# Top-32 attention with a mixture of experts: the second candidate list is sorted down to eight, and three of nine segments give five candidates to the first list

## The chip, the cores and the metric

The kernel runs on one core of one Trainium2 chip. The metric is device time in microseconds (us) of one execution, the median of several runs. Time before: 373.49 us, the median of 3 runs (372.68 to 374.3). A core has a matrix engine (TensorE, PE in the rows, with its weight loads as PEld), a vector engine (VectorE, DVE), a scalar engine (ScalarE, ACT), GpSimd (POOL), SyncE (SP, which issues DMAs here), and 16 DMA engines. Each engine works through its own queue in order and waits on semaphores.

## What is computed

Attention in which each row keeps its 32 largest scores, and then a mixture of experts with one expert per token (8 experts, 1152 tokens):

```
scores = scale * np.matmul(q, k.transpose(0, 1, 3, 2))          # 2 batches, 8 heads, 576 x 576, head size 64
kth = np.partition(scores, -top_k, axis=-1)[..., -top_k:-top_k + 1]   # top_k = 32
scores = np.where(scores >= kth, scores, -1000000000.0)
attn = softmax(scores)
x = np.matmul(attn, v)                     # as 1152 tokens x 512
expert_idx = np.argmax(x @ w_gate, axis=1)
y = np.maximum(x_e @ w1[e], 0.0) @ w2[e]   # per expert e, for its tokens; times the gate's probability
```

## The kernel before

**Units.** Attention is cut into 36 units `u`: 9 tiles of 128 query rows times 4 pairs of heads. A unit holds two score tiles (j = 0, 1) of 128 x 576 in PSUM. Four units make one tile of tokens, which is then routed to the experts.

**How 32 of 576 are found.** `heads` (L285) cuts each row's 576 scores into nine segments of 64 and takes the eight largest of each, sorted, with one MAX8 per segment (L292, 18 per unit), into `un`. The first four of each segment form the first list (36 values), the last four the second list (36 values). `merge` (L299) needs the 16 smallest of the first list and the 16 largest of the second: MAX8 for eight of them (L295 and L305 for the second list into `vb`, L309 for the first into `na`; the first list is read from `nn`, a negated copy), MATCH_REPLACE8 to strike these eight out (L312 second, L315 first; each is a MATCH_VALUE_LOAD and a MATCH_REPLACE8 on the engine), and MAX8 again for the next eight (L317 second, L319 first). With both lists sorted, the 32nd largest of their union is the largest of the minima of pairs: `bound` (L323, in four steps L326, L328, L330, L332) takes twelve pairs per row. Where that bound leaves more than 32 scores above it, up to seven too many are taken away later: `select` (L371) reads the eight smallest kept values with one MAX8 over the row (L380) and picks the threshold.

**Who does what in a unit.** DVE runs `heads`, a reduction that gives the row's maximum (`mx`, L296), `select` of an older unit, and `merge`. ACT makes `nn` from `un` (L336), copies the scores out of PSUM as `sm` = maximum minus score (L339, needs `mx`), takes the exponentials (L417, L408), makes the mask `pen` (L394, needs `nk`, which DVE's L384 writes at the end of `merge`) and the signs that count the kept scores (L349). PE transposes (L415, L416, L406, L407), multiplies by v (L437, L440) and computes the next unit's scores (L277), into the same PSUM tiles that ACT's `sm` copy has to leave first. POOL multiplies for `select` (L356) and splits weights (L616, L618).

**What sets the order.** The order is written by hand. `attention` (L1028) walks over the units; in step i it runs `heads` of unit i, and work of units i-1 to i-9 around it. Small DVE steps (`bound`, parts of `select`, `normalise` L445 with L451, L453, L456 of every second unit, the routing steps) stand in a list `small` and are put between the MAX8 of `heads` and inside `merge`, one at each call of `fill`. In every fourth unit ACT also copies the transposed tokens (L505) and PE runs the gate (L508). After the last unit, from about 240 us, comes the experts' part, bound by weight splits and matrix products.

A repair branch at the end of the program runs the exact selection for everything if any row's bound left fewer than 32 or more than 39 scores.

Of the kernel before, what the change touches and what calls it, by code (L numbers as in the profile page):

```python
# [27 lines left out]
LOW = -3.0e38  # L28
TOPK = 32
SEG = 9  # L30
SPLIT = 256.0


@with_exitstack
def kernel(
# [117 lines left out]


    pd = psum.tile([128, 512], FT, name="pD", bufs=1)
    NB = [pd[:, 24 * i:24 * i + 24].rearrange("p (j c) -> p j c", j=2) for i in range(2)]
    DM = [pd[:, 64 + 16 * i:80 + 16 * i].rearrange("p (j c) -> p j c", j=2) for i in range(2)]
    M1 = [pd[:, 96 + 2 * i:98 + 2 * i] for i in range(2)]
    tab = pd[:, 104:112]
    CG = pd[0:1, 128:256].rearrange("p (i c e) -> p i c e", i=4, c=4)  # L160
    nc.vector.tensor_scalar(tab, e_f, 2.0, float(2 * TOPK - S), op0=OP.mult, op1=OP.add)
    VB = [consts.tile([128, 2, 17], FT, name=f"vb{i}") for i in range(2)]
    for vb in VB:
        nc.vector.memset(vb[:, :, 0:1], -LOW)
    CNT = consts.tile([128, NT * H], FT)
# [114 lines left out]
    def scores_of(u, j):  # L280
        return PS[u][j][:, :S]
# [1 line left out]


    def heads(u, fill):  # L285
        un = work.tile([128, 2, SEG, 8], FT, name="un")
        nn = work.tile([128, 2, SEG, 4], FT, name="nn")
        mx = work.tile([128, 4, 2], FT, name="mx4", bufs=3)
        w = S // SEG
        for j in range(2):  # L290
            for i in range(SEG):
                nc.vector.max(out=un[:, j, i], in_=scores_of(u, j)[:, i * w:(i + 1) * w])  # L292
                if i < SEG - 1:
                    fill()
        nc.vector.max(out=VB[u % 2][:, 0, 1:9], in_=un[:, 0, :, 4:])  # L295
        nc.vector.tensor_reduce(out=mx[:, 0], in_=un[:, :, :, 0], axis=mybir.AxisListType.X, op=OP.max)  # L296
        VAL[u] = [mx, un, nn]

    def merge(u, fill):  # L299
        mx, un, nn = VAL[u]  # L300
        wk = work.tile([128, 2, 2, SEG, 4], FT, name="wk")
        na = work.tile([128, 2, 16], FT, name="na")
        tm = work.tile([128, 2, 12], FT, name="tm")
        vb = VB[u % 2]
        nc.vector.max(out=vb[:, 1, 1:9], in_=un[:, 1, :, 4:])  # L305
        if u == NU - 1:
            fill()
        for j in range(2):
            nc.vector.max(out=na[:, j, 0:8], in_=nn[:, j])  # L309
        fill()  # L310
        for j in range(2):
            nc.vector.match_replace(out=wk[:, 0, j], in_to_replace=vb[:, j, 1:9], in_values=un[:, j, :, 4:],  # L312
                                    imm_value=LOW)
        for j in range(2):
            nc.vector.match_replace(out=wk[:, 1, j], in_to_replace=na[:, j, 0:8], in_values=nn[:, j], imm_value=LOW)  # L315
        for j in range(2):
            nc.vector.max(out=vb[:, j, 9:17], in_=wk[:, 0, j])  # L317
        for j in range(2):
            nc.vector.max(out=na[:, j, 8:16], in_=wk[:, 1, j])  # L319
        fill()  # L320
        VAL[u] = [mx, na, vb, tm]

    def bound(u, step):  # L323
        mx, na, vb, tm = VAL[u]
        if step == 0:
            nc.vector.tensor_scalar(NB[u % 2], na[:, :, 4:16], -1.0, None, op0=OP.mult)  # L326
        elif step == 0.5:
            nc.vector.tensor_tensor(out=tm, in0=NB[u % 2], in1=vb[:, :, 0:12], op=OP.min)  # L328
        elif step == 1:
            nc.vector.tensor_reduce(out=M1[u % 2], in_=tm, axis=mybir.AxisListType.X, op=OP.max)  # L330
        else:
            nc.vector.tensor_sub(mx[:, 2], mx[:, 0], M1[u % 2])  # L332


    def shift(u):
        nc.scalar.activation(VAL[u][2], VAL[u][1][:, :, :, :4], AF.Copy, scale=-1.0)  # L336
        SM[u] = work.tile([128, 2, S], FT, name="sm", tag="sm", bufs=4)
        for j in range(2):
            nc.scalar.activation(SM[u][:, j], scores_of(u, j), AF.Identity, bias=VAL[u][0][:, 0, j:j + 1],  # L339
# [1019 lines left out]
```

## Time and profile before

| what | value |
| --- | --- |
| median of 3 runs | 373.49 us |
| the profiled execution | 375.27 us, of which the span of the program is 373.4 us |
| PE busy | 326.8 us, 88% of the span |
| DVE busy | 321.1 us, 86% |
| ACT busy | 291.9 us, 78% |
| POOL busy | 273.2 us, 73% |

Busy time is a union of an engine's instructions over the whole span; the stages differ, so the shares are to be read per stage. On DVE an instruction's time in the trace overlaps with the next one's start, so what an instruction costs its queue is the distance from its start to the start of the next, and this is the number used below. A figure in brackets at the end of a row is the idle time of that engine just before the instruction, with what ended it.

### The profile page before, as it was taken

How to read it: one execution, taken by the hardware profiler on the slowest of the kernel's cores; microseconds unless marked ns; L12 is line 12 of the kernel's file. 1: busy time of each engine (PE TensorE's matmuls, PEld its weight loads, DVE VectorE, ACT ScalarE, POOL GpSimd, SP SyncE). 2: the span in 40 equal slices, each digit the busy share in tenths (PEclk: the TensorE clock that was granted, in tenths of full speed). 3: DMA queues.
4: the chain of work that ended last, by engine and by line, in shares of the span. 5: the costliest groups of instructions: out<-in, count | busy, mean ns of one | idle time of the engine just before them, and what ended most of it. 6: DMA issues, size and time to landing. Idle time of an engine off the chain costs nothing.

```text
span 373.4 us, 10232 instructions
## 1 busy us (share of the span) xinstructions
PE 326.8 (88%) x3390; PEld 269.4 (72%) x3390; DVE 321.1 (86%) x1863; ACT 291.9 (78%) x573; POOL 273.2 (73%) x293
## 2 busy tenths in 40 slices
PE   5777888988988889888799998999899999898892
PEld 2455666866777768667688887999358978877781
DVE  4889999999999999999999999877863679879820
ACT  5789999999999999998979987765745776677410
POOL 3895969698977789989879999774602578578431
PEclk9778999999999999999989999999999999999897
DMA  9739997936283403030323015394279999999110
GB/s 156 132 72 202 223 196 221 218 113 158 49 254 127 176 32 115 3 141 2 113 58 116 2 37 143 122 351 172 77 224 317 367 324 326 401 334 285 42 32 25
DMA packets 69924, 60.27 MB, mean 161 GB/s; under 512 B 52069, under 2 KB 52069, under 8 KB 69863
## 3 DMA queue, kind: packets, MB, share of 16 engines
q1 hardware_dynamic: 67719, 54.79, 53.7%
q0 software_dynamic: 1616, 4.73, 3.4%
q8 instruction: 28, 0.46, 0.5%
q14 instruction: 33, 0.27, 0.2%
q10 hardware_dynamic: 528, 0.02, 0.1%
HBM read 40.66 MB, written 12.09 MB: 141 GB/s over the span
## 4 chain that ended last, share of the span: by engine, by line
DVE 50%; PE 36%; ACT 5%; issue 4%; DMA 2%; POOL 1%; SPq 1%; POOLq 0%; ACTq 0%
DVE un L292 17%; DVE z L380 10%; PE pS L656 8%; PE pV L440 5%; PE pT L656 4%; PE pD L656 3%; DVE ws L618 3%; DVE wk L315 2%; DVE wk L312 2%; PE pS L277 2%; PE pT L415 2%; PE pT L738 2%; ACT ws L612 2%; DVE vb L317 2%; DVE na L309 1%
## 5 line engine op out<-in xcount | busy, mean ns | idle before, releaser
L292 DVE MAX8 un<-pS 128x8 f32<-128x64 f32 x648 | 109.9, 215 | 1.9 <-PE pS L277 1.3
L356 POOL TENSOR_TENSOR z<-sm,sg 128x576 f32<-128x576 f32 x71 | 89.6, 1282 | 15.0 <-ACT sg L349 14.6
L618 POOL TENSOR_TENSOR ws<-wr,ws 128x1024 bf16<-128x1024 f32 x29 | 66.2, 2289 | 19.7 <-ACT ws L612 18.7
L656 PEld LDWEIGHTS <-ws 128*128 128x128 f16 (+1 forms) x1056 | 71.8, 99 | 6.5 <-issue 4.7
L440 PE MATMUL pV<-vm,pT 128*128 128x65 f32 (+1 forms) x640 | 74.2, 264 | 0.0
L440 PEld LDWEIGHTS pV<-vm,pT 128*128 128x128 f32 (+1 forms) x640 | 70.4, 183 | 0.9 <-issue 0.6
L618 DVE TENSOR_TENSOR ws<-wr,ws 128x1024 bf16<-128x1024 f32 x35 | 60.8, 1766 | 3.8 <-ACT ws L612 3.6
L415 PE MATMUL pT<-ident,sm 128*128 128x128 f32 x288 | 58.9, 286 | 5.5 <-ACT xT L505 1.7
L277 PE MATMUL pS<-qk 128*128 128x512 f16 (+3 forms) x320 | 47.3, 297 | 14.7 <-ACT sm L339 14.7
L416 PE MATMUL pT<-identb,pen 128*128 128x128 bf16 x288 | 53.1, 223 | 5.6 <-ACT pen L394 5.5
L349 ACT ACTIVATE sg<-sm,mx 128x576 bf16<-128x576 f32 x72 | 54.8, 763 | 0.7 <-POOL z L356 0.7
L277 PEld LDWEIGHTS <-qk 128*128 128x128 f16 (+1 forms) x320 | 27.2, 107 | 37.2 <-issue 20.2
L394 ACT ACTIVATE pen<-sm,nk 128x576 bf16<-128x576 f32 x70 | 50.4, 767 | 3.7 <-DVE nk L384 3.3
L380 DVE MAX8 z<-z 128x8 f32<-128x576 f32 x72 | 51.1, 747 | 0.7 <-POOL z L356 0.5
L612 ACT ACTIVATE ws<-wr 128x1024 f16<-128x1024 f32 x50 | 49.8, 1047 | 0.0
L415 PEld LDWEIGHTS pT<-ident,sm 128*128 128x128 f32 x288 | 41.7, 145 | 11.0 <-ACT xT L505 2.9
L339 ACT ACTIVATE sm<-pS,mx 128x576 f32<-128x576 f32 x72 | 49.2, 735 | 0.0
L417 ACT ACTIVATE pT<-pT 128x512 f32<-128x512 f32 x72 | 39.6, 600 | 5.5 <-PE pT L416 5.3
L661 POOL DMA_INDIRECT out_dram<-y,xp x12 | 17.5, 1460 | 27.7 <-ACT y L803 13.5
L416 PEld LDWEIGHTS <-pen 128*128 128x128 bf16 x288 | 29.9, 106 | 9.8 <-ACT pen L394 9.7
L656 PE MATMUL pS<-xe,ws 128*128 128x128 f16 (+2 forms) x336 | 22.8, 226 | 0.0
L542 POOL DMA_INDIRECT xbuf<-xs,ru x9 | 10.0, 1115 | 11.9 <-DVE xs L537 4.0
(256 smaller groups left out, 627.4 us busy)
## 6 DMA issues: line engine op xcount, KB each, us to landing
wr<-in_moe_w_dram SPq DMA_DIRECT2D x32, 1024.0 KB, 6.8
xbuf<-zero SPq DMA_DIRECT2D x6, 771.0 KB, 4.5
qnat<-in_q_dram SPq DMA_DIRECT2D x16, 144.0 KB, 4.0
knat<-in_k_dram SPq DMA_DIRECT2D x16, 144.0 KB, 4.2
out_dram<-zero SPq DMA_DIRECT2D x3, 768.0 KB, 4.6
vm<-in_v_dram SPq DMA_DIRECT2D x16, 128.0 KB, 3.1
qk<-qk SPq DMA_DIRECT2D x14, 144.0 KB, 2.5
vt<-in_v_dram SPq DMA_DIRECT2D x4, 64.0 KB, 3.2
```

Source lines behind the costliest of these rows:

```text
L277: nc.tensor.matmul(PS[u][j][row:row + n, c0:c1], QK[b][2 * i][:, h, s:s + n], QK[b][1][:, h, c0:c1], start=(i == 0), stop=(i == 1))
L292: nc.vector.max(out=un[:, j, i], in_=scores_of(u, j)[:, i * w:(i + 1) * w])
L349: nc.scalar.activation(SG[u][j], SM[u][:, j], AF.Sign, bias=VAL[u][0][:, 2, j:j + 1], scale=-(1.0 - 2.0 ** -20), accum_out=CNT[:, c:c + 1])
L356: engs[j].tensor_tensor(out=Z[u][:, j], in0=SM[u][:, j], in1=SG[u][j], op=OP.mult)
L380: nc.vector.max(out=z8[:, step - 1], in_=Z[u][:, step - 1])
L394: nc.scalar.activation(PEN[u][:, j], SM[u][:, j], AF.Relu, bias=NK[u][:, j:j + 1], scale=BIG)
L415: nc.tensor.matmul(pt[:, c], sm[:, o:o + 128], ident, start=True, stop=False, is_transpose=True)
L416: nc.tensor.matmul(pt[:, c], pen[:, o:o + 128], identb, start=False, stop=True)
L440: nc.tensor.matmul(PV[t][row:row + n, h0 + half], PT[u][:, half, c, row:row + n], VM[b][:, c, p, half], start=False, stop=(half == 1 and c ...
L612: nc.scalar.activation(h[:, d], r[:, s], AF.Copy)
L618: eng.tensor_tensor(out=l[:, d], in0=r[:, s], in1=h[:, d], op=OP.subtract)
L656: nc.tensor.matmul(o, a(i), c(i), start=(i == 0 and m == 0), stop=(i == k - 1 and m == 2))
```

## The change

The second list is now sorted only to its eight largest: L312 and L317 and their tile are gone. Three of the nine segments (the last three; `FOUR = 6` counts the others) give five values to the first list and three to the second. `un` becomes two constant tiles with nine columns per segment: in the first six segments column 0 holds a constant and columns 1 to 8 the eight values; in the last three columns 0 to 7 hold them and column 8 a constant. Columns 0 to 4 are then the first list (45 entries, six of them the constant), columns 5 to 8 the second (36, three of them the constant). The row maximum now stands in column 1 for six segments and in column 0 for three, so it takes two reductions: the first over the six, written into a tenth row of `un`, the second over the last three and that row. `bound` takes nine pairs and not twelve.

```diff
+FOUR = 6
-    NB = [pd[:, 24 * i:24 * i + 24].rearrange("p (j c) -> p j c", j=2) for i in range(2)]
+    NB = [pd[:, 24 * i:24 * i + 18].rearrange("p (j c) -> p j c", j=2) for i in range(2)]
-    VB = [consts.tile([128, 2, 17], FT, name=f"vb{i}") for i in range(2)]
+    VB = [consts.tile([128, 2, 9], FT, name=f"vb{i}") for i in range(2)]
+    UN = [consts.tile([128, 2, SEG + 1, 9], FT, name=f"un{i}") for i in range(2)]
+    for un in UN:
+        nc.gpsimd.memset(un[:, :, :FOUR, 0:1], -LOW)
+        nc.gpsimd.memset(un[:, :, FOUR:SEG, 8:9], LOW)
...
     def heads(u, fill):
-        un = work.tile([128, 2, SEG, 8], FT, name="un")
-        nn = work.tile([128, 2, SEG, 4], FT, name="nn")
+        un = UN[u % 2]
+        nn = work.tile([128, 2, SEG, 5], FT, name="nn")
...
-                nc.vector.max(out=un[:, j, i], in_=scores_of(u, j)[:, i * w:(i + 1) * w])
+                nc.vector.max(out=un[:, j, i, 1:9] if i < FOUR else un[:, j, i, 0:8], in_=scores_of(u, j)[:, i * w:(i + 1) * w])
...
-        nc.vector.max(out=VB[u % 2][:, 0, 1:9], in_=un[:, 0, :, 4:])
-        nc.vector.tensor_reduce(out=mx[:, 0], in_=un[:, :, :, 0], axis=mybir.AxisListType.X, op=OP.max)
+        nc.vector.max(out=VB[u % 2][:, 0, 1:9], in_=un[:, 0, :SEG, 5:9])
+        nc.vector.tensor_reduce(out=un[:, :, SEG, 0], in_=un[:, :, :FOUR, 1], axis=mybir.AxisListType.X, op=OP.max)
+        nc.vector.tensor_reduce(out=mx[:, 0], in_=un[:, :, FOUR:, 0], axis=mybir.AxisListType.X, op=OP.max)
...
     def merge(u, fill):
...
         for j in range(2):
-            nc.vector.match_replace(out=wk[:, 0, j], in_to_replace=vb[:, j, 1:9], in_values=un[:, j, :, 4:],
-                                    imm_value=LOW)
+            nc.vector.match_replace(out=wk[:, j], in_to_replace=na[:, j, 0:8], in_values=nn[:, j], imm_value=LOW)
         for j in range(2):
-            nc.vector.match_replace(out=wk[:, 1, j], in_to_replace=na[:, j, 0:8], in_values=nn[:, j], imm_value=LOW)
-        for j in range(2):
-            nc.vector.max(out=vb[:, j, 9:17], in_=wk[:, 0, j])
-        for j in range(2):
-            nc.vector.max(out=na[:, j, 8:16], in_=wk[:, 1, j])
+            nc.vector.max(out=na[:, j, 8:16], in_=wk[:, j])
...
-            nc.vector.tensor_scalar(NB[u % 2], na[:, :, 4:16], -1.0, None, op0=OP.mult)
+            nc.vector.tensor_scalar(NB[u % 2], na[:, :, 13 - FOUR:22 - FOUR], -1.0, None, op0=OP.mult)
...
-            nc.vector.tensor_tensor(out=tm, in0=NB[u % 2], in1=vb[:, :, 0:12], op=OP.min)
+            nc.vector.tensor_tensor(out=tm, in0=NB[u % 2], in1=vb, op=OP.min)
...
-        nc.scalar.activation(VAL[u][2], VAL[u][1][:, :, :, :4], AF.Copy, scale=-1.0)
+        nc.scalar.activation(VAL[u][2], VAL[u][1][:, :, :SEG, :5], AF.Copy, scale=-1.0)
```

The queue of DVE in a middle unit, from the end of `heads` (the last nine MAX8 over the scores pS) to the first MAX8 of the next unit; the names are the tiles of the text above. Before:

```order
L292 MAX un<-pS_703 128x8 x9
L295 MAX vb_121<-un 128x8
L296 TENSOR_REDUCE mx_739<-un 128x2
L380 MAX z_749<-z 128x8 x2
L305 MAX vb_121<-un 128x8
L309 MAX na<-nn 128x8 x2
L382 SCALAR_TENSOR_TENSOR pD<-pD,z_749 128x16
L312 MATCH_REPLACE wk<-vb_121,un 128x36 x2
L315 MATCH_REPLACE wk<-na,nn 128x36 x2
L317 MAX vb_121<-wk 128x8 x2
L319 MAX na<-wk 128x8 x2
L384 TENSOR_REDUCE nk<-pD 128x2
```

The same place on DVE in the changed kernel, where the lines are numbered anew (L298 is the old L292, L303 the old L296, L382 the old L380, L386 the old L384):

```order
L298 MAX un_123<-pS_697 128x8 x9
L301 MAX vb_121<-un_123 128x8
L302 TENSOR_REDUCE un_123<-un_123 128x2
L303 TENSOR_REDUCE mx_728<-un_123 128x2
L382 MAX z_738<-z 128x8 x2
L312 MAX vb_121<-un_123 128x8
L316 MAX na<-nn 128x8 x2
L384 SCALAR_TENSOR_TENSOR pD<-pD,z_738 128x16
L319 MATCH_REPLACE wk<-na,nn 128x45 x2
L321 MAX na<-wk 128x8 x2
L386 TENSOR_REDUCE nk<-pD 128x2
```

Four instructions of the program left the queue behind L382 (the old L312 and L317, twice each), and one, the new L302, came in ahead of the reduction that writes `mx`; that reduction now reads what the instruction just before it writes.

## Rows read from the trace of the kernel before

**Rows 1.** Busy time by stage: length, then each engine, granted clock, DMA.

```profile
core 0: us, PE busy (x) PEld busy (x) DVE busy (x) ACT busy (x) POOL busy (x), PEclk, DMA share, GB/s
32.00:83.00 51.00, 42.81 (x374) 34.34 (x372) 51.00 (x384) 48.59 (x106) 42.10 (x43) 0.98 0.88 199
83.00:112.00 29.00, 25.16 (x233) 21.36 (x233) 29.00 (x225) 27.11 (x61) 25.02 (x32) 1.00 0.56 148
...
188.00:228.00 40.00, 38.70 (x404) 33.81 (x403) 38.40 (x292) 36.66 (x82) 36.84 (x44) 0.97 0.24 74
...
262.00:373.40 111.40, 98.03 (x1120) 79.86 (x1117) 75.07 (x84) 62.94 (x82) 58.16 (x29) 0.96 0.76 231
```

**Rows 2.** Timeline of DVE, unit 12, reduction and merge: start, length, line, operation.

```profile
86.92 0.18 DVE L296 TENSOR_REDUCE mx<-un 128x2 f32<-128x18 f32 x1
87.02 1.41 DVE L380 MAX8 z<-z 128x8 f32<-128x576 f32 x2
...
88.71 0.08 DVE L312 MATCH_VALUE_LOAD wk<-vb,un 128x8 f32 x1
...
89.04 0.08 DVE L315 MATCH_VALUE_LOAD wk<-na,nn 128x8 f32 x1
...
89.37 0.29 DVE L317 MAX8 vb<-wk 128x8 f32<-128x36 f32 x2
89.57 0.28 DVE L319 MAX8 na<-wk 128x8 f32<-128x36 f32 x2
```

**Rows 3.** Groups of DVE instructions: count, busy us, mean ns, idle before.

```profile
L380 DVE MAX8 z<-z 128x8 f32<-128x576 f32 x72 | 51.1, 747 | 0.7 <-POOL z L356 0.5
...
L317 DVE MAX8 vb<-wk 128x8 f32<-128x36 f32 x72 | 10.3, 184 | 0.0
```

**Rows 4.** Timeline of DVE after the last unit: two steps, each reading the previous.

```profile
240.10 0.19 DVE L326 TENSOR_SCALAR pD<-na 128x24 f32<-128x24 f32 x1
240.32 0.18 DVE L328 TENSOR_TENSOR tm<-pD,vb 128x24 f32<-128x24 f32 x1
```

**Rows 5.** Timeline of ACT, units 12 to 14.

```profile
86.91 0.26 ACT L336 ACTIVATE nn<-un 128x72 f32<-128x72 f32 x1 [0.36 <-DVE un L292]
87.13 1.38 ACT L339 ACTIVATE sm<-pS,mx 128x576 f32<-128x576 f32 x2
...
89.44 0.28 ACT L408 ACTIVATE pTt<-pS 128x128 f32<-128x128 f32 x1
89.95 1.44 ACT L394 ACTIVATE pen<-sm,nk 128x576 bf16<-128x576 f32 x2 [0.23 <-DVE nk L384]
91.30 0.57 ACT L505 ACTIVATE xT<-pT 128x512 f32<-128x512 f32 x1
...
99.41 0.26 ACT L336 ACTIVATE nn<-un 128x72 f32<-128x72 f32 x1 [0.24 <-DVE un L292]
99.63 1.38 ACT L339 ACTIVATE sm<-pS,mx 128x576 f32<-128x576 f32 x2
```

**Rows 6.** Timeline of PE, units 12 to 16: scores, products with v.

```profile
87.92 1.29 PE L277 MATMUL pS<-qk 128*128 128x512 f16 x8 [0.95 <-ACT sm L339]
...
95.85 1.06 PE L440 MATMUL pV<-vm,pT 128*128 128x65 f32 x8
...
107.80 1.06 PE L440 MATMUL pV<-vm,pT 128*128 128x65 f32 x8
```

**Rows 7.** Timeline of DVE: the first step of `normalise` in units 14 and 16.

```profile
96.95 0.16 DVE L451 TENSOR_SCALAR rs<-pV 128x4 f32<-128x4 f32 x1
...
109.45 0.14 DVE L451 TENSOR_SCALAR rs<-pV 128x4 f32<-128x4 f32 x1
```

**Rows 8.** Timeline of PE at 187 us, a product that waited.

```profile
186.84 0.33 PE L415 MATMUL pT<-ident,sm 128*128 128x128 f32 x1 [1.10 <-DVE pD L964]
```

**Rows 9.** Busy times of the stretch behind it; the eighth figure is the granted clock.

```profile
187.28:190.69 3.41, 3.41 (x18) 2.86 (x17) 3.41 (x25) 2.57 (x5) 3.37 (x4) 0.50 0.22 82
```

**Rows 10.** Timeline of DVE at the start: the first maximum of unit 2.

```profile
21.87 0.23 DVE L292 MAX8 un<-pS 128x8 f32<-128x64 f32 x1 [0.46 <-PE pS L277]
```

More of the change, by code (lines that the diff above doesn't have):

```diff
@@ L300, in merge @@
         mx, un, nn = VAL[u]
-        wk = work.tile([128, 2, 2, SEG, 4], FT, name="wk")
+        wk = work.tile([128, 2, SEG, 5], FT, name="wk")
         na = work.tile([128, 2, 16], FT, name="na")
-        tm = work.tile([128, 2, 12], FT, name="tm")
+        tm = work.tile([128, 2, 9], FT, name="tm")
         vb = VB[u % 2]
-        nc.vector.max(out=vb[:, 1, 1:9], in_=un[:, 1, :, 4:])
+        nc.vector.max(out=vb[:, 1, 1:9], in_=un[:, 1, :SEG, 5:9])
         if u == NU - 1:
```

## The prediction

> **What bounds the kernel now.** I read first the busy times by stage [rows 1]. From 32 to 112 us DVE has no idle time at all (51.00 of 51.00 us, 29.00 of 29.00), while ACT is idle for 2.41 and 1.89 us and PE for 8.2 and 3.8. So DVE sets the pace there, with ACT close behind. From 188 to 228 us it is PE that has hardly any idle time, 1.30 us in 40. After 262 us comes the experts' part, which this change does not touch. Second, I read the timelines of the three engines over units 12 to 16, one tile of tokens, to see what becomes late when DVE gets faster [rows 5 to 7]. ACT waits for DVE twice in unit 12, 0.36 us for the end of `heads` and 0.23 us for `nk`. And DVE's L451 in unit 14 starts at 96.95, while the product it reads (L440) ends at 95.85 + 1.06 = 96.91: 0.04 us behind it. That row shows no wait, but it has no room. In unit 16 the same pair is 109.45 against 107.80 + 1.06 = 108.86, 0.59 us of room.
>
> **What the change takes from DVE.** Costs are distances from start to start. The two struck-out copies of the second list (L312) cost 89.04 - 88.71 = 0.33 us per unit, the two MAX8 behind them (L317) 89.57 - 89.37 = 0.20 us [rows 2]. Together 0.53 us.
>
> **What it adds to DVE.** The first list grows from 36 to 45 entries in six instructions (L309, L315, L319, twice each). A MAX8 over 576 entries takes 747 ns and one over 36 takes 184 ns [rows 3], so an entry costs (747 - 184) / 540 = 1.04 ns, and 6 x 9 entries 0.06 us. The reduction for `mx` becomes two, of which the second reads what the first has just written. An independent reduction costs 87.02 - 86.92 = 0.10 us [rows 2]; a step whose next one reads its result costs 240.32 - 240.10 = 0.22 us [rows 4]. The added one is of the second kind. I take 0.20, a little under the row because the first of the two need not wait for the last maximum of `heads`; the bounds are 0.10 and 0.22. Nine pairs in `bound` where there were twelve is 6 entries in three short steps, 0.02 us at 1.04 ns, and I leave it out. Net per unit: 0.53 - 0.06 - 0.20 = 0.27 us, between 0.25 and 0.37. Over 36 units that is 9.7 us of DVE's time.
>
> The Trainium skill, in "VectorE: DVE Perf Modes" (The DRAIN you can't avoid; Rules for kernel authors), says that semaphores between DVE instructions cost nothing extra and that only their count matters. Rows 4 against rows 2 (0.22 against 0.10) speak against it here. By the page the net would be 0.37 us per unit and the sum below 1.6 us more (368.0 us: 0.5 in units 3 to 8, 0.1 at the start, 0.2 in each of five tiles).
>
> **What it moves on the other engines.** `nn` on ACT grows from 72 to 90 entries, about 0.02 us at the same price per entry, hidden where ACT waits for `mx` anyway and else paid on ACT, 36 x 0.02 = 0.7 us at most. Four memsets on POOL stand in the set-up, before its first products, where it waits for loads; none of them is on a path, and without that cover they would cost four short fills once. The order of instructions on PE, ACT and SP is unchanged, so nothing is queued behind a new wait except on DVE itself: behind the dependent reduction stand `select`'s L380, `merge` and the next `heads`, which is the 0.20 above, and ACT's `sm` waits for it. That is the second price: `mx` comes 0.20 us later after the end of `heads`, wherever ACT was already waiting. `sm` frees the PSUM tiles for the next scores, so PE waits that much longer too.
>
> **Where DVE's gain gets through.** I follow the tile of units 12 to 16 from the end of `heads` of unit 12 (86.9).
>
> Units 12 to 14: `sm` starts 0.20 later than 87.13. ACT's queue then carries the delay to L408 (89.44) and to `pen`. `pen` had waited 0.23 for `nk`, and `nk` now comes 0.27 earlier. ACT's next instruction starts about 0.09 before the end of the one ahead (89.95 + 1.44 = 91.39, L505 at 91.30), so `pen` can start at 89.44 + 0.20 + 0.28 - 0.09 = 89.83 instead of 89.95: 0.12 earlier. From L505 on the way runs over PE (gate, products, scores, L440) to L451, which had 0.04 us of room. So L451, and with it the end of `heads` of unit 14, gains 0.12, and not the 2 x 0.27 = 0.54 that DVE could.
>
> Units 14 to 16: DVE would bring L451 forward by 0.12 + 0.54 = 0.66, to 108.79. On ACT, `nn` starts at 99.41 - 0.12 = 99.29 and `sm` 0.42 later (0.22 before, 0.20 for `mx`), at 99.71 instead of 99.63. L440 then ends at 108.86 + 0.08 = 108.94, and L451 starts at 108.98: 0.47 earlier than before. So a tile gains about 0.47 us of the 1.08 that DVE saves in it.
>
> The sum. Units 0 to 2: DVE waits there for PE's scores (0.46 us before unit 2 [rows 10]), which wait for `sm`: a loss of 0.2, once. Units 3 to 8, before the first tile is routed: ACT has the room, DVE sets the pace, 5 x 0.27 = 1.4. Units 8 to 28, five tiles: 5 x 0.47 = 2.35. Units 28 to 35: PE is full, so between nothing and the 1.30 us that it idles; nearest to nothing, 0.3. The experts' part only starts earlier. Together 1.4 + 2.35 + 0.3 - 0.2 = 3.9 us. The profiled execution (375.27 us) would come to 371.4; it lies 1.78 us above the median of the runs, so the median would be 373.49 - 3.9 = 369.6 us.
>
> **Rivals.**
>
> Full landing. DVE is the engine with no idle time, ACT and PE make room, and nearly all of its 9.7 us arrives: 373.5 - 9.7 = 363.8 us, or 366 with part of units 28 to 35 lost. For it speaks that DVE has no idle time in 80 us on end; against it the 0.04 us at L451 and PE's 38.70 of 40.00 us. This is what the Trainium skill's "Perfetto Trace Analysis" (Identifying the Most-Contended Engine) would lead to: it has the engine of highest occupancy optimized first. The trace agrees on which engine that is, but not that it alone decides. Chance 0.22.
>
> Nothing lands. The later `mx` costs on ACT's and PE's way what DVE saves: if `pen` does not start earlier, a tile's first half loses up to 0.2 and its second half gains 0.2 to 0.3, and only units 3 to 8 are left: 371.6 to 374 us. For it speaks that ACT is 94 to 95% busy; against it the 0.23 us that ACT waits for `nk`, which the change removes. Chance 0.20.
>
> Slower, by the clock. The granted clock fell to half (1.2 GHz) from 187.28 to 190.69, right after PE had waited 1.10 us in one piece [rows 8, 9]. In that stretch PE lost 3.41 / 2 = 1.7 us of work at 2.4 GHz. PE waits 0.95 us for `sm` in unit 12 [rows 6], and with `mx` later this grows to 1.15. If that longer wait brings such a stretch once per tile, that is five times 1.7 = 8.5 us against a gain of 3.9: 378 us. It decides from three stretches on (5.1 us). Against it speaks that PE waited 0.95 us in unit 12 and the clock stayed at 1.00 from 83 to 112 us. Chance 0.06.
>
> It doesn't do what it says. With eight of the second list the bound can be weaker, so that more scores pass; above 39 the repair branch runs. Counted on the reference's own inputs, the largest count is 39 (37 before). So the branch stays closed, but with one row at its edge. It would redo all 36 units, well over 100 us. Chance 0.01.
>
> **How the numbers follow.** The forecast, 367 to 371.5 us, has 0.51. The time is that of the forecast, 369.6. The range takes in half of the full landing below and most of "nothing lands" above: 365.3 to 372.9. About 0.5% (1.9 us) is what a measurement of this kernel can tell from no change. Faster by more, under 371.6: the forecast's 0.51 and full landing's 0.22, 0.73. Within it: 0.20. Slower: 0.07.
>
> **What would show it.** Right: in units 3 to 8 the distance between two reductions for `mx` falls by about 0.27 us and DVE still has no idle time; in the tiles DVE has new idle time before L451, ended by PE's L440, of 0.2 to 0.4 us; the wait of `pen` for `nk` is gone and `sm` starts on the end of `mx`; the two reductions lie 0.2 us apart. Wrong: if DVE shows no new waits from 83 to 112 us, the gain lands whole; if the distance of the two reductions is 0.10, the price of the dependent step was wrong; if the granted clock falls below 1.00 between 83 and 112 us, the third rival holds.

## The result and the profile after

The median went from 373.98 us (372.68 to 376.92, 20 runs) to 370.38 us (368.21 to 373.38, 20 runs). The ratio is 0.9904, with a 95% interval of 0.9881 to 0.9928: faster by 0.7 to 1.2%, 3.6 us. The forecast was 369.6 us and 3.9 us faster. As a sum that is close; stage by stage it is not, as will be seen.

The profiled execution of after took 369.16 us, with a span of 367.4 us; that of before 375.27 and 373.4. So the two profiles stand 6.1 us apart and the two medians 3.6. Stage times below are of the two profiled executions, and what in them belongs to the clock has to be taken out before they are held against the medians.

The page of after first: busy time of each engine, and the chain of work that ended last by engine.

```profile
PE 324.0 (88%) x3390; PEld 267.9 (73%) x3390; DVE 309.6 (84%) x1683; ACT 290.9 (79%) x573; POOL 274.7 (75%) x297
...
PE 49%; DVE 29%; ACT 13%; issue 4%; DMA 2%; SPq 1%; POOL 1%; ACTq 0%; POOLq 0%
```

DVE has 180 instructions fewer (1683 for 1863) and 11.5 us less to do (309.6 for 321.1). In before the same chain was 50% DVE, 36% PE and 5% ACT. More of it now runs over PE and ACT. That does not make DVE idle: it is still the busiest engine of the tiles, as the third row below shows.

Busy time of after by stage: length, PE, weight loads, DVE, ACT, POOL, granted clock, DMA share, GB/s. The windows are those of [rows 1], with one more from 62 to 190 us, which holds most of the tiles.

```profile
32.00:83.00 51.00, 44.42 (x370) 35.67 (x370) 48.96 (x347) 48.06 (x105) 41.96 (x43) 0.93 0.90 199
83.00:112.00 29.00, 25.55 (x240) 21.79 (x240) 28.49 (x202) 28.03 (x63) 26.16 (x33) 1.00 0.58 153
62.00:190.00 128.00, 114.20 (x1105) 94.72 (x1103) 125.26 (x912) 122.36 (x268) 113.75 (x132) 1.00 0.42 116
188.00:228.00 40.00, 38.65 (x430) 34.13 (x429) 37.24 (x262) 36.05 (x83) 37.94 (x47) 1.00 0.27 75
262.00:367.30 105.30, 91.59 (x1096) 76.27 (x1094) 70.62 (x66) 58.98 (x77) 55.49 (x27) 0.99 0.81 241
```

DVE, which had no idle time at all in the first two, now idles 2.04 and 0.51 us there. From 188 to 228 us it idles 2.76 us where it had idled 1.60.

In after's code the line numbers stand 2 to 6 higher: L298 is the maximum over a segment (L292 before), L302 the added reduction, L303 the one for `mx` (L296), L341 `sm`, L396 `pen`, L442 the products with v (L440), L453 the first step of `normalise` (L451). L507 and L521 belong to the routing of a finished tile (the copy of the transposed tokens, the first step behind the gate). The kernels of the experiments are shifted by a few lines more; what a line is there is said where it is shown.

DVE of after in unit 12, the rows that answer [rows 2] and [rows 4].

```profile
86.06 0.17 DVE L301 MAX8 vb<-un 128x8 f32<-128x36 f32 x1
86.16 0.15 DVE L302 TENSOR_REDUCE un<-un 128x2 f32<-128x12 f32 x1
86.34 0.17 DVE L303 TENSOR_REDUCE mx<-un 128x2 f32<-128x8 f32 x1
86.43 1.41 DVE L382 MAX8 z<-z 128x8 f32<-128x576 f32 x2
...
88.49 0.33 DVE L321 MAX8 na<-wk 128x8 f32<-128x45 f32 x2
```

From L302 to L303 there are 0.18 us, from L303 to the next, independent instruction 0.09. The added, dependent reduction costs 0.18 where 0.20 was taken. The copies and the two MAX8 of the second list are gone.

ACT of after in unit 12, against [rows 5], and the first steps of `normalise` on DVE, against [rows 7].

```profile
86.17 0.28 ACT L338 ACTIVATE nn<-un 128x90 f32<-128x90 f32 x1
86.55 1.37 ACT L341 ACTIVATE sm<-pS,mx 128x576 f32<-128x576 f32 x2
...
89.03 1.43 ACT L396 ACTIVATE pen<-sm,nk 128x576 bf16<-128x576 f32 x2
90.36 0.58 ACT L507 ACTIVATE xT<-pT 128x512 f32<-128x512 f32 x1
```

```profile
96.02 0.16 DVE L453 TENSOR_SCALAR rs<-pV 128x4 f32<-128x4 f32 x1 [0.30 <-PE pV L442]
...
107.98 0.16 DVE L453 TENSOR_SCALAR rs<-pV 128x4 f32<-128x4 f32 x1
```

`sm` starts at 86.55, right behind the end of `mx` at 86.34 + 0.17 = 86.51. `pen` no longer waits for `nk`. And DVE has the wait that was looked for: L453 waits 0.30 us for L442 in unit 14. The same wait of 0.27 to 0.34 us stands in units 6, 10, 14, 22, 26, 30, 32 and 34. It is not new everywhere: before the change it stood already in units 22, 30 and 34, as here in unit 22. New are those of units 6, 10, 14, 26 and 32.

```profile
147.37 0.16 DVE L451 TENSOR_SCALAR rs<-pV 128x4 f32<-128x4 f32 x1 [0.28 <-PE pV L440]
```

What DVE saves can be read from units in which it waits for nobody: from the end of one `heads` to the end of the next, unit 13 took 5.82 us before and takes 5.51 now. That is 0.31 us, where 0.27 was forecast.

The stages of the two profiled executions, marked by the end of the last segment maximum of a unit (so "3 to 8" runs from the end of `heads` of unit 3 to that of unit 8); us:

| stage | before | after | difference | forecast |
|---|---|---|---|---|
| units 3 to 8 | 30.05 | 30.11 | +0.06 | -1.4 |
| 8 to 12 | 24.77 | 23.95 | -0.82 | -0.47 |
| 12 to 16 | 24.76 | 24.05 | -0.71 | -0.47 |
| 16 to 20 | 25.37 | 24.66 | -0.71 | -0.47 |
| 20 to 24 | 25.06 | 24.25 | -0.81 | -0.47 |
| 24 to 28 | 25.68 | 24.88 | -0.80 | -0.47 |
| 28 to 35 | 50.62 | 49.07 | -1.55 | -0.3 |
| behind 35 | 134.99 | 134.33 | -0.66 | 0 |

Two stages stand out. Units 3 to 8, where DVE had set the pace alone, won nothing. The stage 28 to 35, where PE is full, won 1.55 us. The granted clock has to do with both. Here are two windows of after, the columns as above; then the instruction of PE that ended the idle time there, and the one of DVE that waited for PE behind it.

```profile
33.46:40.29 6.83, 6.01 (x32) 4.24 (x31) 6.80 (x51) 5.99 (x14) 4.04 (x5) 0.50 1.06 184
31.20:33.46 2.26, 0.19 (x3) 0.10 (x1) 2.23 (x12) 1.96 (x5) 2.12 (x2) 1.00 0.98 221
```

```profile
33.33 1.98 PE L283 MATMUL pS<-qk 128*128 128x512 f16 x8 [2.07 <-ACT sm L341]
```

```profile
41.46 0.23 DVE L298 MAX8 un<-pS 128x8 f32<-128x64 f32 x1 [1.13 <-PE pS L283]
```

PE waited 2.07 us for `sm`, and from 33.46 on the granted clock was 0.50 (1.2 GHz) for 6.83 us. DVE then waited 1.13 us for scores. In before the stretch of [rows 9] lay at 187.28; after has none there (units 16 to 35 run at 1.00).

### The profile page after: what moved, and what is told of

Read it like the earlier page. It is cut to its first block, busy times and chain, and to the rows that moved or that the text cites. A ratio compares the mean times of both kernels' runs of the same rounds, so it can differ in the third digit from the quotient of the medians.

```text
span 367.4 us, 10058 instructions
## 1 busy us (share of the span) xinstructions
PE 324.0 (88%) x3390; PEld 267.9 (73%) x3390; DVE 309.6 (84%) x1683; ACT 290.9 (79%) x573; POOL 274.7 (75%) x297
## 4 chain that ended last, share of the span: by engine, by line
PE 49%; DVE 29%; ACT 13%; issue 4%; DMA 2%; SPq 1%; POOL 1%; ACTq 0%; POOLq 0%
DVE un L298 12%; PE pV L442 8%; PE pS L658 8%; PE pS L283 6%; PE pT L658 5%; DVE z L382 4%; PE pT L417 4%; ACT sm L341 3%; PE pD L658 3%; DVE ws L620 3%; ACT pen L396 2%; PE pT L740 2%; PE pT L418 2%; ACT ws L614 2%; ACT pT L419 2%
## 5 line engine op out<-in xcount | busy, mean ns | idle before, releaser
L298 DVE MAX8 un<-pS 128x8 f32<-128x64 f32 x648 | 109.8, 216 | 4.4 <-PE pS L283 3.6
L358 POOL TENSOR_TENSOR z<-sm,sg 128x576 f32<-128x576 f32 x71 | 89.6, 1280 | 14.3 <-ACT sg L351 14.1
L658 PEld LDWEIGHTS <-ws 128*128 128x128 f16 (+1 forms) x1056 | 70.3, 98 | 6.6 <-issue 4.7
L442 PE MATMUL pV<-vm,pT 128*128 128x65 f32 (+1 forms) x640 | 73.7, 263 | 0.0
L442 PEld LDWEIGHTS pV<-vm,pT 128*128 128x128 f32 (+1 forms) x640 | 70.0, 182 | 0.9 <-issue 0.6
L351 ACT ACTIVATE sg<-sm,mx 128x576 bf16<-128x576 f32 x72 | 54.9, 766 | 1.0 <-POOL z L358 1.0
L382 DVE MAX8 z<-z 128x8 f32<-128x576 f32 x72 | 51.1, 747 | 1.3 <-POOL z L358 1.1
L341 ACT ACTIVATE sm<-pS,mx 128x576 f32<-128x576 f32 x72 | 49.1, 734 | 1.4
L396 ACT ACTIVATE pen<-sm,nk 128x576 bf16<-128x576 f32 x70 | 50.2, 766 | 0.0
L663 POOL DMA_INDIRECT out_dram<-y,xp x12 | 18.6, 1548 | 26.4 <-ACT y L805 12.7
L439 PE MATMUL pV<-vt,pTt 128*128 128x130 f32 (+1 forms) x80 | 18.1, 308 | 0.0
```

Source lines behind the costliest of these rows:

```text
L298: nc.vector.max(out=un[:, j, i, 1:9] if i < FOUR else un[:, j, i, 0:8], in_=scores_of(u, j)[:, i * w:(i + 1) * w])
L358: engs[j].tensor_tensor(out=Z[u][:, j], in0=SM[u][:, j], in1=SG[u][j], op=OP.mult)
L382: nc.vector.max(out=z8[:, step - 1], in_=Z[u][:, step - 1])
L396: nc.scalar.activation(PEN[u][:, j], SM[u][:, j], AF.Relu, bias=NK[u][:, j:j + 1], scale=BIG)
L442: nc.tensor.matmul(PV[t][row:row + n, h0 + half], PT[u][:, half, c, row:row + n], VM[b][:, c, p, half], start=False, stop=(half == 1 and c ...
L658: nc.tensor.matmul(o, a(i), c(i), start=(i == 0 and m == 0), stop=(i == k - 1 and m == 2))
```

## Experiments

### Each part alone

The change has two parts, the shorter second list and the fifth candidate of three segments. The first two kernels take them apart.

The second list shortened, four candidates everywhere. The diff is held against the changed kernel; the kernel is the one before with the changes to the second list alone.

```diff
-                nc.vector.max(out=un[:, j, i, 1:9] if i < FOUR else un[:, j, i, 0:8], in_=...)
+                nc.vector.max(out=un[:, j, i], in_=...)
-        nc.vector.tensor_reduce(out=un[:, :, SEG, 0], in_=un[:, :, :FOUR, 1], ...)
-        nc.vector.tensor_reduce(out=mx[:, 0], in_=un[:, :, FOUR:, 0], ...)
+        nc.vector.tensor_reduce(out=mx[:, 0], in_=un[:, :, :, 0], ...)
```

> The second list sorted to eight and nothing else: four candidates from every segment, one reduction for mx, 36 entries. Theory (after the first tile is routed, each tile of four units runs at the pace of the way from the end of heads over ACT's sm and pen, xT and PE's products to L451; DVE's saving lands only where that way is shorter too): mx is not later, pen's wait for nk (0.23 us) goes, so a tile gains about 0.3 us in its first half and 0.55 in its second, some 0.9 to 1.2, against 0.8 in the changed kernel; units 3 to 8 gain 0.55 each. Sum 7 to 9 us: 365 to 367 us, and L451 waits for PE's L440 in the tiles. Rival (DVE's busy time alone decides): 36 x 0.55 = 20 us, 354 us, and no wait at L451.

Measured: 367.9 us (367.33 to 369.36) against 374.59 of before, ratio 0.9812 (0.9772 to 0.9852): 6.7 us faster, a little under what was expected and more than the change as a whole. The rival, 354 us, fell. Counted on the reference's inputs, its largest count is 39 too, so the repair branch stays closed. The tiles from unit 16 on took 24.32, 23.87 and 24.33 us, 0.34 to 0.55 less than after. But tile 12 to 16 took 26.30 us, 1.54 more than before the change. DVE and POOL of that kernel show why (L375 is the MAX8 over `z`, L351 POOL's product that makes `z`, L199 POOL's first step on the second batch's q):

```profile
89.19 0.76 DVE L375 MAX8 z<-z 128x8 f32<-128x576 f32 x1 [0.41 <-POOL z L351]
90.42 0.76 DVE L375 MAX8 z<-z 128x8 f32<-128x576 f32 x1 [0.47 <-POOL z L351]
```

```profile
70.03 0.83 POOL L199 TENSOR_SCALAR hl<-qnat 96x768 f16<-96x768 f32 x1 [2.76 <-DMA qnat<-in_q_dram]
```

DVE came to `z` before POOL had it, and POOL had waited 2.76 us for a load at 70 us; that the one comes from the other is tested below with the loads. DVE had overtaken the next supplier.

The other part alone: the changed kernel with the second list's second sort put back, its result unused.

```diff
         for j in range(2):
+            nc.vector.match_replace(out=wx[:, j], in_to_replace=vb[:, j, 1:9], in_values=un[:, j, :SEG, 5:9], imm_value=LOW)
+        for j in range(2):
             nc.vector.match_replace(out=wk[:, j], ...)
...
+            nc.vector.max(out=v2[:, j], in_=wx[:, j])
```

> The changed kernel with the second list's further eight sorted again, into a tile that nobody reads: the additions of the change without its saving. DVE pays 0.53 us per unit more than in the changed kernel, 0.25 us more than before. Theory: DVE then sets the pace everywhere up to unit 28, so the addition lands nearly whole: 25 x 0.25 = 6 to 7 us over the time before, with a little more at the start, 380 to 382 us; against the changed kernel that is 10 us, two to three times what taking the same work away brought. Rival (saving and adding are worth the same at this place): 3.6 us over the changed kernel, 374 us, no different from before.

Measured: 379.93 us (379.23 to 383.23), ratio 1.0148 (1.0101 to 1.0196): as the theory said, and the rival, 374 us, fell. DVE of that kernel, the two struck-out copies and the two MAX8, and the busy times from 62 to 190 us:

```profile
91.09 0.08 DVE L321 MATCH_VALUE_LOAD wx<-vb,un 128x8 f32 x1
...
91.42 0.08 DVE L323 MATCH_VALUE_LOAD wk<-na,nn 128x8 f32 x1
...
91.77 0.29 DVE L325 MAX8 v<-wx 128x8 f32<-128x36 f32 x2
91.97 0.30 DVE L327 MAX8 na<-wk 128x8 f32<-128x45 f32 x2
```

```profile
62.00:190.00 128.00, 109.18 (x1051) 89.66 (x1049) 127.02 (x974) 117.79 (x254) 107.56 (x124) 1.00 0.41 114
```

The price of the second sort is as forecast, 0.33 + 0.20 = 0.53 us a unit. Without it the changed kernel is 9.1 us faster (ratio 0.9904 in place of 1.0148, of 374 us), half of 36 x 0.53 = 19 us. And with DVE almost full (127.02 of 128 us), what the fifth candidates add can be read by itself: a tile takes 0.67 to 0.81 us more than before, 0.17 to 0.20 us a unit, where 0.26 was forecast.

### When the row maximum comes

The first reduction put between the maxima, so that only the second stands behind them:

```diff
+                if j and i == FOUR:
+                    nc.vector.tensor_reduce(out=un[:, :, SEG, 0], in_=un[:, :, :FOUR, 1], ...)
...
-        nc.vector.tensor_reduce(out=un[:, :, SEG, 0], in_=un[:, :, :FOUR, 1], ...)
```

> The changed kernel with the first of the two reductions moved up between the maxima of the last segments, so that the second no longer follows directly on what it reads. Theory (the dependent step costs 0.12 us of DVE and, what weighs more, brings sm 0.2 us later where ACT waits for it): the distance from the last maximum of heads to sm shrinks by about 0.2 us, a tile gains 0.2 to 0.3 us more than in the changed kernel, units 3 to 8 gain 0.1 each: 1.5 to 2.5 us faster than the changed kernel, 368 to 369 us. Rival (the later mx costs nothing, since the wait at L451 sets the pace whenever sm starts): 0.1 us per unit in units 3 to 8 and nothing in the tiles, 0.5 us, not to be seen.

Measured: 369.56 us (367.41 to 371.24), ratio 0.9841 (0.9798 to 0.9883): against after 0.8 us by the medians and 2.4 by the two ratios, whose intervals touch, so the size is not settled. DVE and ACT of that kernel at unit 12 (L302 is the first reduction, L304 the one for `mx`, L342 `sm`):

```profile
83.93 0.16 DVE L302 TENSOR_REDUCE un<-un 128x2 f32<-128x12 f32 x1
84.00 0.35 DVE L298 MAX8 un<-pS 128x8 f32<-128x64 f32 x2
...
84.39 0.17 DVE L304 TENSOR_REDUCE mx<-un 128x2 f32<-128x8 f32 x1
```

```profile
85.22 1.35 ACT L342 ACTIVATE sm<-pS,mx 128x576 f32<-128x576 f32 x2
```

The reduction is followed after 0.07 us when the next instruction does not read it. Where ACT has nothing else to do first, `sm` starts 0.23 us behind the end of `heads` where it was 0.41, and the tiles from unit 16 on take 0.18 to 0.26 us less than after. In this unit `sm` is late for another reason, and tile 12 to 16 took 26.29 us, with DVE waiting for POOL's `z` as in the first kernel. So part of what was won elsewhere was lost in that tile.

The opposite: one MAX8 over `z` put ahead of the two reductions. DVE does the same work; `mx` comes 0.63 us later.

```diff
+        for f, *a in pre:
+            f(*a)
         nc.vector.tensor_reduce(out=un[:, :, SEG, 0], in_=un[:, :, :FOUR, 1], ...)
...
-            run(at(3, penalty) + copies() + at(0, heads, fill))
+            run(at(3, penalty) + copies() + at(0, heads, fill, at(2, select, 1)))
...
-            run(mid.get(i, []) + at(2, select, 1) + at(2, select, 2))
+            run(mid.get(i, []) + at(2, select, 2))
```

> The changed kernel with one of the two MAX8 over z (128x576, about 0.63 us) moved ahead of the two reductions that give the row maximum. VectorE does the same instructions; only the maximum, and with it ACT's subtraction and the next scores, come 0.63 us later in each unit. Theory: since the changed kernel has VectorE waiting for TensorE in every second or fourth unit, the way of a unit over ACT and TensorE has become a bound of its own there. Next scores were ready 0.8 us ahead of VectorE in most units and 0.04 us in units 10, 14, 22, 26, 30 and 34: 0.6 us is lost in those six and 0.3 to 0.6 in as many others, 4 to 7 us in all, 374 to 377 us. Rival: VectorE's work alone sets the time, 370 to 371 us.

Measured: 383.87 us (383.06 to 384.3), ratio 1.024 (1.0213 to 1.0267), which by the two ratios is 12.6 us slower than after. DVE of that kernel, with the new wait; then the group of segment maxima in it; then two windows.

```profile
72.91 0.23 DVE L298 MAX8 un<-pS 128x8 f32<-128x64 f32 x1 [0.69 <-PE pS L283]
```

```profile
L298 DVE MAX8 un<-pS 128x8 f32<-128x64 f32 x648 | 110.5, 218 | 11.7 <-PE pS L283 11.0 <-ACT qk L243 0.7
```

```profile
79.30:86.10 6.80, 6.80 (x40) 5.61 (x39) 5.50 (x40) 5.66 (x15) 6.33 (x8) 0.50 0.22 43
106.60:113.40 6.80, 6.80 (x40) 5.60 (x38) 5.50 (x40) 5.66 (x15) 6.32 (x7) 0.50 0.73 204
```

The kind of loss is as the theory said, the size is not: 4 to 7 us were expected. The rival, no loss, fell. Tiles 8 to 12 and 12 to 16, which hold the two windows at half clock, lost 3.31 and 3.49 us; the next three lost 1.90, 1.28 and 1.10. From unit 3 to 35 the two profiles differ by 14.1 us; had the first two tiles lost 1.5 us each, near the mean of the other three, it would be 10.3. So by this estimate nearly 4 us of the loss belong to the clock.

The same move in the kernel before the change:

> The kernel before the change with one MAX8 over z (0.63 us) moved ahead of the reduction that gives the row maximum; VectorE's work is the same. In the changed kernel this cost 13 us, 4.4 of them in two tiles that got stretches of half clock. Theory: here VectorE is the bound and the next scores lie 1.26 us ahead of it in most units, 0.33 or 0.04 us in units 10, 14, 22, 26, 29, 30 and 34; 0.63 us later costs 0.3 to 0.6 us in those seven, 3 to 5 us in all, 377.5 to 379.5 us: less than half of what it cost after the change, because the change took the cover. Rival: the way over ACT and TensorE was as much a bound before; 385 us or more.

Measured: 377.44 us (376.04 to 381.91), ratio 1.0094 (1.0056 to 1.0133), by the ratio 3.5 us slower. The theory holds, at the lower edge. The same 0.63 us a unit cost 3.5 us before the change and 12.6 after it. The clock does not explain the difference: in the three tiles from unit 16 to 28, where none of the four kernels ran at half clock (but for the last 0.5 us of before), the loss was 0.55, 0.18 and 0.22 us before the change and 1.90, 1.28 and 1.10 after it, 0.95 against 4.28 us. Before, DVE's work covered most of it; after, the way from `mx` over ACT and PE back to DVE has much less cover. That is shown with no instruction added or removed.

### Where `normalise` waits

`normalise` of the changed kernel put behind the routing steps in the list that fills the gaps of `heads`.

```diff
-            small += at(5, normalise, 0) + at(5, normalise, 1) + at(5, normalise, 2) + routes((2, 2.1, 2.2, 4, 5, 5.5)) + late.get(i, [])
+            small += routes((2, 2.1, 2.2, 4, 5, 5.5)) + at(5, normalise, 0) + at(5, normalise, 1) + at(5, normalise, 2) + late.get(i, [])
```

> The changed kernel with normalise (L451 first) moved behind the routing steps in the list of small DVE steps, so that it comes two or three maxima later in every unit in which both stand. Theory (L451 waits 0.30 us for PE's L440 in units 10, 14, 22, 26 and 30, and that wait clips DVE's gain): the wait goes, a tile gains up to 0.25 us more until ACT or the next scores stop DVE, 1 to 1.5 us in all against the changed kernel, 369 us. Rival (the wait is only where the lag shows, and ACT and PE set the pace in any case): DVE's idle time moves to the scores (L298) or to na, and the time stays at the changed kernel's 370.4 us.

Measured: 369.56 us (369.04 to 371.45), ratio 0.9869 (0.9826 to 0.9911). The wait did not go, it changed its place. DVE of that kernel, unit 10:

```profile
72.05 0.17 DVE L521 COPY r<-pV 128x8 f32<-128x8 f32 x1 [0.30 <-PE pV L442]
...
72.88 0.14 DVE L453 TENSOR_SCALAR rs<-pV 128x4 f32<-128x4 f32 x1
```

The routing's first step reads what PE makes behind the same products, and waits for it 0.30 us. So the theory failed. The tiles from unit 16 on are those of after (24.58, 24.25, 24.88 us), and tile 12 to 16 took 0.51 us more: the loss is PE's lateness, not the place where DVE meets it. Against after the time is 0.8 us less by the medians, which these stages do not show.

### The clock at 33 us, and the loads

Extra matmuls into spare columns where PE stood idle ahead of the scores of units 3 and 4:

```diff
+            for n in range({2: 28, 3: 36}.get(i, 0)):
+                nc.tensor.matmul(pv[:, 392:512], identb, onesb[:, :120], start=True, stop=True)
             half, nxt = at(4, values, 1), at(-1, scores)
```

> The changed kernel with 28 and 36 extra matmuls of 120 columns into spare columns, where TensorE stands idle ahead of the scores of units 3 and 4 (1.58 us before 28.5 us and 2.07 us before 33.3 us). Theory: units 3 to 8 took as long as before the change because TensorE ran at half clock from 33.5 to 40.3 us; with the idle time filled that stretch does not come, the stage falls from 30.1 to between 28.0 and 29.0 us, and the time by 1.1 to 2.1 us against the changed kernel, to 368.3 to 369.3 us. Rival: the half clock comes all the same, or the stage is bound by ACT there; 30.1 us and 370.4 us stay.

Measured: 371.12 us (370.51 to 372.17), ratio 0.9908 (0.9881 to 0.9936), so no gain against after. The same two windows as in after, POOL's step on q, and DVE's MAX8 over `z`:

```profile
31.20:33.46 2.26, 2.14 (x40) 2.01 (x39) 2.23 (x14) 1.96 (x7) 1.93 (x2) 1.00 0.77 169
33.46:40.29 6.83, 5.41 (x46) 3.90 (x46) 6.79 (x50) 6.83 (x16) 3.36 (x4) 1.00 1.17 202
```

```profile
71.84 0.83 POOL L205 TENSOR_SCALAR hl<-qnat 96x768 f16<-96x768 f32 x1 [2.86 <-DMA qnat<-in_q_dram]
```

```profile
92.26 0.76 DVE L382 MAX8 z<-z 128x8 f32<-128x576 f32 x1 [0.47 <-POOL z L358]
```

The stage did what the theory said: no half clock, and units 3 to 8 in 28.55 us, 1.50 less than before the change, where 1.4 had been forecast. But tile 12 to 16 took 26.34 us in place of 24.05. Whoever comes to unit 8 early meets the late load, and pays it back. The kernel with the shorter second list alone and the one with the early reduction had that too: no half clock from 32 to 62 us, 27.70 and 28.09 us there, and 26.3 in tile 12 to 16.

So the loads next. In the kernel with the shorter second list alone the load of q was issued at 66.2 us, behind the transposes of the pair before. Issued one unit earlier:

```diff
             if i == 0 and p:
-                side.setdefault(at - 2, []).append((load_qk, 1, p))
+                side.setdefault(at - 3, []).append((load_qk, 1, p))
```

> The kernel with the shorter second list alone (four candidates everywhere), and in it each load of q and k of the second batch issued one unit earlier, so that on SP it stands ahead of the transposes of the pair before, for which it had to wait. Theory: the bad tile of that kernel (units 12 to 16 in 26.30 us, its neighbours in 24.1 and 24.3) came from POOL, which waited 2.76 us at 67.3 us for a load issued at 66.2 us behind two transposes and fell behind by that; with the load earlier the wait goes and the tile comes down to 24.1 to 24.4, so 365.5 to 366.2 us. Rival: the transposes and the clearing writes hold the 16 DMA engines then, the load lands no sooner or something else falls behind, and the time stays at 367.5 to 368.5.

Measured: 367.8 us (364.31 to 369.63), ratio 0.98 (0.9756 to 0.9844). The tile came down to 23.97 us, a little more than expected, and POOL had no wait for that load any more. But the profiled execution had a new loss. A window of that kernel, and DVE behind it:

```profile
33.30:40.10 6.80, 5.98 (x34) 4.61 (x32) 6.14 (x48) 6.20 (x14) 4.32 (x6) 0.50 1.03 196
```

```profile
40.92 0.23 DVE L292 MAX8 un<-pS 128x8 f32<-128x64 f32 x1 [1.48 <-PE pS L277]
```

Half clock, as in after, and 29.66 us for units 3 to 8. The theory held for the tile and failed for the time, which stayed where it was. Its runs spread over 5.3 us. Both helps together, on the shorter second list alone:

> The shorter second list alone, with the loads one unit earlier and the extra matmuls ahead of the scores of units 3 and 4. Theory: both gains add, since they are in different stages: tile 12 to 16 at 24.1 to 24.4 us; units 3 to 8 of that kernel had no half clock after 31.1 us, so the matmuls give 0 to 0.5 us; 365.0 to 366.2 us. Rival: as in the kernel without the matmuls but with the loads, or, if the loads do nothing, 367.5 to 368.5.

Measured: 365.63 us (364.49 to 368.08), ratio 0.9765 (0.9731 to 0.9799), the fastest here, 8.9 us under before. Units 3 to 8 took 27.72, tile 12 to 16 24.40 us: both gains stand side by side, as the theory said. Both helps on the changed kernel, and on the kernel before:

> The changed kernel with both helps: loads of q and k of the second batch one unit earlier, and the extra matmuls ahead of the scores of units 3 and 4. With the matmuls alone units 3 to 8 came down by 1.6 us to 28.55, and tile 12 to 16 went up by 2.3 us to 26.34, since VectorE came there before POOL had z. Theory: what was won ahead of unit 8 was given back to late loads; with the loads early the tile goes back to 24.0 to 24.4 and the time to 368.0 to 369.0 us. Rival: the tile is bound by something else than these loads and stays at 26.3; 371 us.

> The kernel before the change with the same two helps, so that the change can be taken with both sides helped. Theory: VectorE's own work bounds units 3 to 28 there (5.82 us a unit, no idle time), so the loads give nothing and the matmuls at most 0.9 us (units 3 to 8 from 30.05 to 29.2 us): 373.5 to 374.6 us, and the change is then worth 5 to 6.5 us in place of 3.6. Rival: the helps are worth as much to both kernels; 371 to 372 us, and the change is worth 3 to 4 us.

Measured for the changed kernel: 369.88 us, ratio 0.985 (0.9792 to 0.9908), above the 368 to 369 expected. Units 3 to 8 came to 28.51 us, but tile 12 to 16 only to 25.31. POOL there waits for the transposes now, no longer for the load:

```profile
59.75 0.83 POOL L205 TENSOR_SCALAR hl<-knat 96x768 f16<-96x768 f32 x1 [0.74 <-DMA qk<-hl]
...
70.32 0.83 POOL L205 TENSOR_SCALAR hl<-qnat 96x768 f16<-96x768 f32 x1 [0.94 <-DMA qk<-hl]
```

The theory held by half; what holds the rest of this tile back was not tried further. Measured for the kernel before: 374.37 us (372.98 to 378.21), ratio 1.0006 (0.997 to 1.0042), nothing, as the theory said. A window of it:

```profile
31.00:62.00 31.00, 26.19 (x257) 21.59 (x255) 31.00 (x235) 29.60 (x64) 24.19 (x22) 1.00 1.03 200
```

DVE is busy 31.00 of 31.00 us, and units 3 to 8 take 30.05 us as they did without the helps. With the helps on both sides the change is worth 374.37 - 369.88 = 4.5 us by the medians and 5.8 by the two ratios, against 5 to 6.5 expected; the first of the two intervals is wide. This kernel also gives the price of the half clock elsewhere, since its profiled execution had none before 366 us: units 28 to 35 took 49.57 us in place of 50.62, and the part behind unit 35 took 133.78 in place of 134.99.

## Why the prediction was right, and where it was not

**DVE's saving.** Right. The second sort costs 0.53 us a unit, as measured where it was put back. The additions were taken at 0.26 and measured 0.17 to 0.20, with 0.18 for the dependent reduction in place of 0.20; so the longer list cost less than the 0.06 forecast, and the net saving of 0.31 lies a little above 0.27. The price of dependence is real: the same reduction is followed after 0.18 us by one that reads it and after 0.07 us by one that does not. The Trainium skill's "VectorE: DVE Perf Modes" (The DRAIN you can't avoid; Rules for kernel authors) says that semaphores between DVE instructions cost nothing extra and that their count is what matters; 0.18 against 0.07 us does not agree with that.

**Units 3 to 8, forecast 1.4 us, got nothing.** The saving per unit was right; the assumption that DVE sets the pace there was not. With PE kept busy the stage came to 28.55 us, 1.50 less than before. In after, PE waited 2.07 us for `sm`, and the granted clock fell to half behind that. The prediction had such a rival ("slower, by the clock"), but put it into the tiles, where the clock stayed at 1.00, and not at the start, where PE's waits are longest (2.07 us; behind 40 us none of after is over 1.00). Before the change the stage took the same 30.05 us with a stretch of half clock at its start and without one, but that stretch was short (30.26 to 33.68 us) and the stage began at 32.06. The kernel with the second sort put back shows the cover better. It ran at half clock for 10.2 us, as this window of it shows, and lost about 0.2 us: its unit 5 took 6.23 us, and a unit without waits 6.02. In after the same unit took 6.73, and a unit without waits 5.51.

```profile
30.30:40.50 10.20, 8.54 (x46) 6.04 (x47) 10.13 (x73) 9.21 (x21) 5.84 (x8) 0.50 1.01 187
```

**Tiles, forecast 0.47 us each, got 0.71 to 0.82.** The mechanism is the one forecast: a first half that gains little, a second that gains more, a wait before L453 at the end of most first halves. For units 12 to 14 the gain is 12.50 - 12.31 = 0.19 (forecast 0.12), for 14 to 16 it is 12.26 - 11.74 = 0.52 (0.35). By single units: three of the four win DVE's whole saving of 0.31, or nearly, and the one that meets the wait loses 0.12 (unit 14, 6.80 for 6.68). The step that failed is the price of the later `mx` in the second half. The forecast carried it the whole way: L440's end 0.20 us later against the end of `heads` of unit 14. `sm` was later, by 0.16 (98.86 - 98.45 = 0.41, before 99.63 - 99.38 = 0.25). But L442 ended 107.95 - 98.45 = 9.50 us behind `heads` and L440 108.86 - 99.38 = 9.48: only 0.02 of it arrived. ACT's `sm` of units 14 and 15 and `nn` of unit 15, and PE's L442, of after first; then `nn` and `sm` of unit 15 before the change.

```profile
98.86 1.37 ACT L341 ACTIVATE sm<-pS,mx 128x576 f32<-128x576 f32 x2
...
104.47 0.27 ACT L338 ACTIVATE nn<-un 128x90 f32<-128x90 f32 x1
104.65 1.35 ACT L341 ACTIVATE sm<-pS,mx 128x576 f32<-128x576 f32 x2
...
106.89 1.06 PE L442 MATMUL pV<-vm,pT 128*128 128x65 f32 x8
```

```profile
105.32 0.26 ACT L336 ACTIVATE nn<-un 128x72 f32<-128x72 f32 x1
105.53 1.38 ACT L339 ACTIVATE sm<-pS,mx 128x576 f32<-128x576 f32 x2
```

From `sm` of unit 14 to `sm` of unit 15 ACT took 104.65 - 98.86 = 5.79 us, before 105.53 - 99.63 = 5.90 [rows 5]: 0.11 of the 0.16 went there, 0.03 of it between `nn` and `sm` (0.18 us for 0.21). In unit 15 ACT came to `nn` 0.42 us behind the end of `heads` (104.05), so there the later `mx` cost nothing. So an ACT queue that is 96% busy (122.36 of 128 us from 62 to 190 us) still took up most of 0.16 us on the way through a pair. It did not take up 0.63 us a unit.

**Units 28 to 35, forecast 0.3, got 1.55.** About 1.05 of it is the half clock of [rows 9] that did not come in after, by the kernel before with both helps, which did without it: 50.62 - 49.57. The change itself gave 49.57 - 49.07 = 0.50. Behind unit 35, where 0 was forecast, the comparison without the half clock at 348 us stands at 133.78 before and 134.33 after: 0.55 lost. Five experiments with the shorter second list that kept their clock there took 133.93 to 134.37, so it is not this one execution alone; the cause stays open.

**The sum.** 3.9 was forecast and 3.6 measured, but by errors that cancel, and that they cancel is luck: 1.5 us less than forecast in units 3 to 8, 1.5 more in the tiles, 0.2 more in units 28 to 35, 0.55 less behind them. The loss of 0.2 at the start was 0.1 (units 0 to 3 in 17.68 us, before 17.59).

**Rivals.** Full landing fell: DVE's 9.7 us did not arrive, and other limits came up: in after the clock at the start and the way over ACT and PE, and in the kernels that come to unit 8 earlier also the loads that POOL waits for. The Trainium skill's "Perfetto Trace Analysis" (Identifying the Most-Contended Engine) has the engine of highest occupancy optimized first; how much of it can be won, it does not say. From 32 to 112 us, where DVE had no idle time, that was the right engine, and 3.6 of its 9.7 us were won. "Nothing lands" fell by the tiles. The clock did cost in after, in one place and not in the five tiles. The repair branch stayed closed.

## What to carry to other kernels

Work taken from an engine with no idle time is gained only until the next supplier is late, and there may be several of them close behind, each in its own stage: take the stages apart before you sum. To see whether a loop over other engines has become the bound, delay its first result without adding work (one instruction moved); if that costs several times what it did before, most of the cover is gone; take stages at half clock out of the comparison first. When a stage wins and a later one loses the same amount, look for a load whose time of issue is fixed by a queue and not by the work.

## What the runs showed that was not expected

The half clock moves with small changes, and its price depends on what covers it. A wait of PE does not bring it by itself. The kernel before with both helps had the same 1.10 us wait as [rows 8], and kept its clock; after had 0.94 us at the same place, and kept it too. PE of the kernel before with both helps:

```profile
187.39 0.33 PE L415 MATMUL pT<-ident,sm 128*128 128x128 f32 x1 [1.10 <-DVE pD L964]
```

What decides it stays open. Its price in units 28 to 35 was 1.05 us for 3.4 us at half clock, and in the experts' part, where it came at 341 to 348 us in several kernels, about 1.2 us (134.99 against 133.78). In units 3 to 8 it was about 1.5 us after the change (30.11 against 28.55), for 6.83 us, and about 0.2 us for 10.2 us where the second sort had been put back.

The shorter second list without the fifth candidates was faster than the change itself, by 2.5 us by the medians and 3.4 by the ratios. On these inputs the largest count is 39 with either; whether the fifth candidates are needed on others was not looked at.
